# Chosen buffers, eight planned weight chunks and tiles at multiples of 1024 bytes, in an attention and two-layer MLP kernel

## The chip, the cores and the metric

The kernel runs on one core of a Trainium2 chip. The metric is the device time in microseconds (us): the median of three runs before the change is 821.01 us (820.14 to 821.43). The instructions of a core stand in separate queues, one for each engine: TensorE (PE in the rows, with its weight loads as PEld), VectorE (DVE), ScalarE (ACT), GpSimd (POOL) and SyncE (SP), which here issues every DMA. Each engine takes its queue in order.

## The reference

Two batches of eight heads (16 heads in all, of 768 tokens by 64) go through attention in which a query sees only the keys whose six hash bits are the same as its own:

```
mask = q_bucket[:, :, :, None] == k_bucket[:, :, None, :]
scores = scale * np.matmul(q, k.transpose(0, 1, 3, 2))
scores = np.where(mask, scores, -1000000000.0)
attn = exp(scores - max); attn = attn / (sum(attn) + 1e-09)
x = attn @ v                      # 1536 tokens x 512
x = leaky(x @ w_in) @ w_out       # 512 -> 2048 -> 512
h = x @ w_in2;  out = (h * cos(h)) @ w_out2
```

## The kernel before

To keep float32 accuracy, each operand of a matmul is split into a rounded high part (ACT writes it) and a low part, operand minus high part, which DVE or POOL writes.

**Attention.** For each of the 16 heads PE computes hash bits (`bits_mm`, line 268), masked scores for a row maximum (`max_mm`, 284, reduced by DVE in line 290), scores again (`qk`, 361 and 362) and, for each of six key blocks, the product with V (`pv`, 396). Between the last two stand the exponential and the split of its result. A table `LO` of letters chooses the way of each block. At a G, ACT writes exp to `pf` (371) and rounds it to `ph` (379), and POOL subtracts (383). At a V, ACT writes exp to `ph` (368) and once more into PSUM (376), and DVE subtracts (383). `st` is a ring of three PSUM buffers that all of these scores use; a V block holds its buffer until the subtraction is done.

**The MLP.** 96 steps (2 layers, 4 groups of 4 blocks of hidden units, 3 token blocks of 512) each have 12 matmuls of 512 columns for `h` (655), an activation on ACT and DVE, and 12 matmuls for `y` (700), which stand some steps later in PE's order. The weights come as 32 chunks of 1 MB, one for each block of hidden units in a layer, each of them used by three steps. A chunk arrives as 64-bit words and is turned into a high and a low float part in seven pieces (`stages`, 560): ACT (580), four on DVE (581, 582, 583, 573), ACT for the high part (584), POOL for the low part (577). Eight chunks are held at a time: six in the former tiles `at0` to `at3` of attention, two (numbers 6 and 7, and later 14, 15 and so on) in `wx0` to `wx3`.

**What sets the order.** `Plan` is a list scheduler: each piece of work has an engine, a cost, predecessors and a priority (`KEY`, `FIX`, `CHUNK_KEY`), and `order` writes each engine's queue from them. All of attention, the first twelve `h` steps, the first nine `y` steps and the first six weight chunks (`CHUNKS`) go through it. After that `rest` (745) writes the steps in a fixed rhythm, and `tick` (598) starts one piece of weight work in each step. The planner takes a ring's buffers in turn, and a tile pool gives them out in turn.

Of the kernel before, what the change touches and what calls it, by code (L numbers as in the profile page):

```python
# [18 lines left out]
NH = B * H  # L19
# [11 lines left out]
LO = [{0: 'GGGGGG', 1: 'VGVGVV', 2: 'GVGGVG', 12: 'GGGVGV', 13: 'GVGGGG', 14: 'VGVVGV', 15: 'GGVGVV'}.get(n, "VGGGVG") for n in range(NH)]  # L31
CHUNKS = 6
# [3 lines left out]
    load=-118, hi=-28, d2=-23, d3=18, lo=-83, dl=-28, bm=-14.2, bw=-32, db2=-57, db1=-38, mm=-8.1, mr=-25,  # L36
    rt=-10, fl=82, neg=-50, dr=-48, de=-28, qk=0.8, ex=-6, cv=-29, sub=-21, pe=86, pv=4.7, pw=3.2, ev=-15,
    lc=10, rc=27, dw=-3, rr=-17, xm=56, xh=57, xl=20, vload=5, vh=25, vl=1, sv=-10.3, sh=101, sl=26, wload=58,
    w0=45, w1=73, w2=10, w3=62, w4=-37, w5=99, w6=-57, mi=-5, ga=-8, gm=-40, gh=80, gl=-47, mo=56, ye=2,
)  # L40
FIX = {
# [7 lines left out]
}  # L49
CHUNK_KEY = (95.9, 69.7, 115.6, 142.2, 66.7, 109.6, 173.8, 129.6)  # L50
# [3 lines left out]
    mm=0.351, mr=0.953, rt=0.12, fl=0.45, dr=0.75, de=1.3, neg=0.65, qk=0.702, ex=0.81, cv=0.84, subV=0.95, subG=1.87,  # L54
    pe=0.351, pv=0.702, pw=0.351, ev=0.83, lc=0.55, rc=0.18, dw=0.45, rr=0.55, xm=1.85, xh=0.83, xl=1.87,
    vload=0.6, vh=0.83, vl=1.87, sv=1.37, sh=0.75, sl=0.4,
    wload=0.4, w0=1.11, w1=0.69, w2=0.69, w3=0.95, w4=0.95, w5=0.93, w6=2.37,
    hi0=0.52, lo0=0.52, k2=0.83, idt=0.5, bm0=1.0, bw0=0.69, kb0=0.52,
    mi=2.73, ga=0.63, gm=0.68, gh=0.63, glV=0.65, glG=1.3, mo=2.73, ye=0.65,
# [34 lines left out]
class Plan:  # L94
# [4 lines left out]
    def __init__(self, rings, free):  # L99
        self.rings, self.free = rings, dict(free)  # L100
        self.items, self.index = [], {}

    def add(self, name, e, kind, key, fn, after=(), take=None, give=(), cost=None, moe=False):
        deps = [self.index[d] for d in after if d is not None and d in self.index]
        it = dict(name=name, e=e, kind=kind, key=(key, len(self.items)), fn=fn, deps=deps, take=take, give=list(give),
                  cost=COST[kind] if cost is None else cost, out=[], left=len(deps), moe=moe, before=[])
        for d in deps:
            d["out"].append(it)
        self.items.append(it)
        self.index[name] = it  # L110

    def order(self):
        free = {e: self.free.get(e, 0.0) for e in "PVAGQ"}
        ready = {e: [] for e in "PVAGQ"}
        taken = {r: [] for r in self.rings}
# [7 lines left out]
        def start(it):  # L123
            t = max(free[it["e"]], it["at"])
            r = it["take"]
            if r is not None:
                n = len(taken[r]) - self.rings[r]
                if n >= 0:
                    t = max(t, taken[r][n].get("end", 1e9))
            return t  # L130

        while len(done) < len(self.items):
# [26 lines left out]
            if it["take"] is not None:  # L159
                it["slot"] = {}  # L160
                taken[it["take"]].append(it["slot"])
                n = len(taken[it["take"]]) - 1 - self.rings[it["take"]]
                it["before"] = [taken[it["take"]][n]["by"]] if n >= 0 else []
            for g in it["give"]:
                self.index[g]["slot"].update(end=end + 0.06, by=it)
# [9 lines left out]

def attention(tc, ctx, plan, xp, dr_p, XH, XL, AT, VH, VL, YX, qkt, v, proj, cst, fd, more_raws, heads=NH):

    nc = tc.nc
    T, V, A, G, Q = nc.tensor, nc.vector, nc.scalar, nc.gpsimd, nc.sync
    if True:  # L180
        pool = lambda n, b, **kw: ctx.enter_context(tc.tile_pool(name=n, bufs=b, **kw))
        con = pool("con", 1)
        raw_p = pool("raw", 2)
        vraw_p = pool("vraw", 1)
        phi_p = pool("phi", 3)
        plo_p = pool("plo", 3)
        pf_p = pool("pf", 2)
        sm_p = pool("sm", 3)
        sv_p = pool("svp", 1)
        st_ps = pool("st", 3, space=bass.MemoryType.PSUM)  # L190
        pv_ps = pool("pvp", 1, space=bass.MemoryType.PSUM)
        OS = [YX[:, i * S:(i + 1) * S] for i in range(2)]
        RR, XX = (YX[:, i * S:(i + 1) * S] for i in (2, 3))
        LC, RC = (xp.tile([128, 4, C], F32, name=n) for n in ("lc", "rc"))
# [6 lines left out]
        raw = {0: raw_p.tile([128, S], F32, name="raw")}  # L201
# [5 lines left out]
        E = [con.tile([128, S], F32R, name=f"e{i}") for i in range(2)]  # L207
        SV = [con.tile([128, 4, 128], F32R, name=f"sv{i}") for i in range(2)]
# [12 lines left out]
        neg = con.tile([1, S], F32, name="neg")  # L221
        G.memset(neg, -1.0)
        ident = con.tile([128, 128], F32R, name="ident")
# [21 lines left out]
        def load_qk(n):  # L245
            raw[n] = raw_p.tile([128, S], F32, name="raw")
# [33 lines left out]
        def max_mm(n, t):  # L280
            at = AT[n % NR]
            ps = st_ps.tile([128, 2, 512], F32, name="st")
# [4 lines left out]
        def max_red(n, t):  # L287
            if n not in mx:
                mx[n] = sm_p.tile([128, C], F32R, name="mx")
            V.reduce_max(mx[n][:, t:t + 1], mps.pop((n, t))[:, :, 0:HS], axis=AX.XY)  # L290

        def row_mm(n):
            rps[n] = st_ps.tile([128, 2, 512], F32, name="st")
            T.matmul(rps[n][0:C, 0, 0:128], mx.pop(n), ident, start=True, stop=True)

        def row_fin(n):
            ps = rps.pop(n)[0:C, 0, 0:128]
            mts[n] = sm_p.tile([C, 2, 128], F32, name="mt")
# [15 lines left out]
        def load_v(g):  # L314
            vraw[g] = vraw_p.tile([128, C, 4, 64], F32, name="vraw")
# [12 lines left out]
        def sum_v(g):  # L328
            ps = st_ps.tile([128, 2, 512], F32, name="st")
# [11 lines left out]
        def sum_vh(g):  # L341
            ps, dst = sv_parts(g)
            svp[g, 1] = sv_p.tile([128, 2, 2, 64], F32R, name="svt")
# [11 lines left out]
        def qk(n, k):  # L355
            at = AT[n % NR]
            ps = st_ps.tile([128, 2, 512], F32, name="st")
# [7 lines left out]
        def exp(n, k):  # L365
            if LO[n][k] == "V":
                phi[n, k] = phi_p.tile([128, S], F32R, name="ph")
                A.activation(halves(phi[n, k]), sps[n, k], AF.Exp, scale=SCALE)
            else:
                pf[n, k] = halves(pf_p.tile([128, S], F32, name="pf"))  # L370
                A.activation(pf[n, k], sps.pop((n, k)), AF.Exp, scale=SCALE)  # L371

        def exp_cv(n, k):
# [27 lines left out]
        drs = {}  # L401
# [11 lines left out]
        def dr_dma(n):  # L413
            drs[n] = dr_p.tile([1, S], F32, name="dr")
            Q.dma_start(drs[n].rearrange("o (p c) -> (o p) c", c=C), RC[:, n % 4])

        def rr_dma(n):
            r = n % 2 * 64
            Q.dma_start(RR[r:r + 64], drs.pop(n).to_broadcast([64, S]))
# [34 lines left out]
        for h in range(2):  # L454
            plan.add(("hi0", h), "A", "hi0", -40, lambda h=h: hi0(h))
            plan.add(("lo0", h), "V", "lo0", -40, lambda h=h: lo0(h), [("hi0", h)])
# [12 lines left out]
        for n in range(heads):  # L469
# [4 lines left out]
            if n:  # L474
                do("load", n, "Q", load_qk, n, take="raw" if n > 1 else None, after=[("load", n - 1), ("dr", n - 3)])
# [3 lines left out]
                do("lo", n, "G", lo, n, after=[("hi", n)], give=[("load", n)] if n > 1 else ())  # L479
# [41 lines left out]
            do("lc", n, "Q", lc_dma, n, take="lc", after=[("ev", n)])  # L521
            do("rc", n, "V", recip, n, take="rc", after=[("lc", n)], give=[("lc", n)])
            do("dw", n, "Q", dr_dma, n, after=[("rc", n)], give=[("rc", n)])
# [13 lines left out]
        tiles = [[(c * 2 + i) // 3 for i in range(2)] for c in range(CHUNKS)]  # L537
        for c in range(CHUNKS):
            key = CHUNK_KEY[c]
            do("wload", c, "Q", wload, c, key=key - 8, after=[("pw", 11, C - 1), ("wload", c - 1), ("w4", c - 2)])  # L540
            readers = [(x, 12 + t, k) for t in tiles[c] for x in ("qk", "mm") for k in range(C)]
            for j, e in enumerate("AVVVVAG"):
                do(f"w{j}", c, e, fd.piece, c, j, key=key, take="wsc" if j == 0 else None, give=[("w0", c)] if j == 6 else (),
                   after=[("wload", c)] if j == 0 else [(f"w{j - 1}", c)] + (readers if j == 5 else []))


class Weights:


    def __init__(self, tc, sc_pool, src, raws, parts):  # L550
        self.tc, self.src, self.sc_p = tc, src, sc_pool
# [8 lines left out]
    def stages(self, c):  # L560
# [6 lines left out]
        sc = self.sc_p.tile([128, 2 * KT * 128], F32, name="wsc")  # L567
# [54 lines left out]
class Moe:  # L622


    def __init__(self, tc, XH, XL, W, fd, out, YX):
# [3 lines left out]
        self.h, self.gs, self.ys, self.open = {}, {}, {}, None  # L629

    def begin(self, ctx):
        pool = lambda n, b, **kw: ctx.enter_context(self.tc.tile_pool(name=n, bufs=b, reuse_waits="tile", **kw))
        self.t_p = pool("t", 2)
        self.g_p = pool("g", LAG + 1)
        y_p = pool("ysb", 1)
        self.h_ps = pool("h", 4, space=bass.MemoryType.PSUM)
        self.y_ps = pool("y", 1, space=bass.MemoryType.PSUM)
# [9 lines left out]
    def mm_in(self, s):  # L647
        b = self.steps[s][2]
        ps = self.h[s] = self.h_ps.tile([128, TB], F32, name="h")
# [8 lines left out]
    def act(self, s):  # L658
        nc, ps = self.tc.nc, self.h[s]
        g = self.gs[s] = self.t_p.tile([128, TB], F32, name="gf")  # L660
        if self.steps[s][0] == 0:
            nc.scalar.activation(g, ps, AF.Copy, scale=0.01)  # L662
        else:

            ki = self.t_p.tile([128, TB], I32, name="ki")
# [12 lines left out]
    def high(self, s):  # L678
        gh = self.g_p.tile([128, TB], F32R, name="gh")
        gl = self.g_p.tile([128, TB], F32R, name="gl")  # L680
# [9 lines left out]
    def mm_out(self, s):  # L690
# [4 lines left out]
        if j == 0:  # L695
            self.ys[l, b] = [self.y_ps.tile([128, TB], F32, name=f"y{e}") for e in range(KT)]
        for e in range(KT):
            y = self.ys[l, b][e]
# [160 lines left out]
```

## Time and profile before

| | us |
|---|---|
| median of 3 runs | 821.01 |
| the profiled execution's own time | 821.24 |
| its span, from first to last instruction | 819.4 |
| busy: PE / DVE / ACT / POOL | 786.8 / 479.5 / 438.4 / 432.4 |
| first `h` matmul of the MLP starts at | 264.84 |
| last matmul starts at | 815.25 |

A step's length is read from the distance of the starts of its first matmuls, since the durations of single matmuls overlap.

### The profile page before, as it was taken

To read this page: it belongs to the slowest core of one execution; us is meant where nothing else is said; L and a number is where in the kernel's file an instruction comes from. 1 tells how busy PE (TensorE), PEld (TensorE's weight loads), DVE (VectorE), ACT (ScalarE), POOL (GpSimd) and SP (SyncE) were. 2 spreads that over 40 slices of the span, in tenths; PEclk is the share of its full clock that TensorE was granted. 3 is DMA by queue.
4 is the path that set the end of the run, shared out by engine and by line. 5 is a ranking of instruction groups with operands and counts; after the bars stand their busy time and mean duration, and the time that the engine had idled before them with its cause. 6 is when DMAs were issued, how large, how long until landed. Compare 5 with 4: busy or idle time off the path is not lost. (4 is left out here: it accounts for less than half of the span.)

```text
span 819.4 us, 9862 instructions
## 1 busy us (share of the span) xinstructions
PE 786.8 (96%) x3648; PEld 667.8 (81%) x3648; DVE 479.5 (59%) x579; ACT 438.4 (53%) x630; POOL 432.4 (53%) x282
## 2 busy tenths in 40 slices
PE   6999999999899999779999999999999999999998
PEld 4899999989799788558888888887788888888886
DVE  7666666656777952337666356456747737743333
ACT  3777878867789424224333224355656555544442
POOL 8768887977778512223455334846623533532221
PEclk9999999999999999889999999999999999999999
DMA  6534534524531610112222112102202210000012
GB/s 177 149 84 111 147 91 102 138 64 109 167 110 57 215 68 1 52 52 90 70 98 103 52 52 102 52 4 100 102 1 66 89 52 1 0 1 2 0 52 103
DMA packets 24264, 63.19 MB, mean 77 GB/s; under 512 B 7684, under 2 KB 11428, under 8 KB 20120
## 3 DMA queue, kind: packets, MB, share of 16 engines
q1 hardware_dynamic: 24216, 62.56, 25.1%
q8 instruction: 29, 0.48, 0.2%
q14 instruction: 19, 0.16, 0.1%
HBM read 46.21 MB, written 3.19 MB: 60 GB/s over the span
## 5 line engine op out<-in xcount | busy, mean ns | idle before, releaser
L687 POOL TENSOR_TENSOR gl<-gf,gh 128x512 fp32r<-128x512 f32 x88 | 123.1, 1399 | 298.8 <-ACT gh L681 238.0
L700 PE MATMUL y<-gh,at 128*128 128x512 f32 x576 | 181.0, 395 | 1.6 <-ACT ys L709 1.6
L655 PE MATMUL h<-XH,at 128*128 128x512 f32 x576 | 143.9, 391 | 0.0
L383 POOL TENSOR_TENSOR pl<-pf,ph 128x768 fp32r<-128x768 f32 x62 | 116.3, 1884 | 40.1 <-ACT ph L379 33.3
L700 PEld LDWEIGHTS y<-gh,at 128*128 128x128 f32 x576 | 107.6, 187 | 28.1 <-ACT ys L709 2.0
L655 PEld LDWEIGHTS h<-XH,at 128*128 128x128 f32 x576 | 108.0, 188 | 24.9 <-POOL at L577 0.5
L290 DVE TENSOR_REDUCE mx<-st 128x1 fp32r<-128x768 f32 x96 | 90.9, 956 | 43.4 <-PE st L284 41.4
L700 PE MATMUL y<-gl,at 128*128 128x512 f32 x288 | 113.6, 395 | 0.7 <-POOL gl L687 0.7
L662 ACT ACTIVATE gf<-h 128x512 f32<-128x512 f32 x48 | 28.7, 598 | 143.1 <-PE h L655 127.0
L672 DVE TENSOR_TENSOR gf<-h,gf 128x512 f32<-128x512 f32 x48 | 33.1, 690 | 108.7 <-ACT gf L662 108.6
L666 ACT ACTIVATE ki<-h 128x512 int32<-128x512 f32 x48 | 28.7, 598 | 107.1 <-PE h L655 107.1
L655 PE MATMUL h<-XL,at 128*128 128x512 f32 x288 | 77.0, 389 | 0.0
L667 DVE SCALAR_TENSOR_TENSOR gf<-ki,h 128x512 f32<-128x512 int32 x48 | 33.0, 687 | 72.9 <-ACT ki L666 66.9
L361 PE MATMUL st<-at 77*128 77x384 f32 x192 | 67.4, 351 | 3.8 <-DVE mx L290 2.3
L700 PEld LDWEIGHTS y<-gl,at 128*128 128x128 f32 x288 | 53.9, 187 | 14.3 <-POOL gl L687 1.1
L362 PE MATMUL st<-at 128*128 128x384 f32 x192 | 65.2, 340 | 0.0
L577 POOL TENSOR_TENSOR at<-wsc,at 128x1024 fp32r<-128x1024 f32 x24 | 60.3, 2512 | 7.1 <-ACT at L584 7.1
L655 PE MATMUL h<-XH,wx 128*128 128x512 f32 x192 | 52.6, 417 | 11.2 <-ACT wx L584 10.5
L655 PEld LDWEIGHTS h<-XL,at 128*128 128x128 f32 x288 | 54.1, 188 | 11.4
L681 ACT ACTIVATE gh<-gf 128x512 fp32r<-128x512 f32 x96 | 59.8, 623 | 4.0 <-DVE gf L672 2.3
L371 ACT ACTIVATE pf<-st 128x768 f32<-128x768 f32 x62 | 50.1, 808 | 19.3 <-PE st L362 17.6
L676 DVE SCALAR_TENSOR_TENSOR gf<-gf,h 128x512 f32<-128x512 f32 x48 | 32.9, 685 | 46.2 <-ACT gf L675 46.2
(95 smaller groups left out, 1467.1 us busy)
## 6 DMA issues: line engine op xcount, KB each, us to landing
wrvh<-in_w_dram SPq DMA_DIRECT2D x16, 1024.0 KB
wrvl<-in_w_dram SPq DMA_DIRECT2D x16, 1024.0 KB
at<-at SPq DMA_DIRECT2D x63, 192.0 KB
raw<-in_qk_dram SPq DMA_DIRECT2D x15, 384.0 KB
vraw<-in_v_dram SPq DMA_DIRECT2D x4, 768.0 KB
yx<-dr SPq DMA_DIRECT2D x16, 192.0 KB
out_dram<-ys SPq DMA_DIRECT2D x6, 256.0 KB
out_dram<-yx SPq DMA_DIRECT2D x6, 256.0 KB
```

Source lines behind the costliest of these rows:

```text
L290: V.reduce_max(mx[n][:, t:t + 1], mps.pop((n, t))[:, :, 0:HS], axis=AX.XY)
L361: T.matmul(o, at[0:R76 + 1, 2, kc], at[0:R76 + 1, 0, COL[h]], start=True, stop=False)
L362: T.matmul(o, at[:, 3, kc], at[:, 1, COL[h]], start=False, stop=True)
L371: A.activation(pf[n, k], sps.pop((n, k)), AF.Exp, scale=SCALE)
L383: (V if LO[n][k] == "V" else G).tensor_tensor(halves(plo[n, k]), pf.pop((n, k)), halves(f32(phi[n, k])), op=ALU.subtract)
L577: G.tensor_tensor(lf, sc, f32(hf), op=ALU.subtract)
L655: self.tc.nc.tensor.matmul(ps, w[:, 0, k], x[:, k, cols], start=(j == 0), stop=(j == 3 * KT - 1))
L667: nc.vector.scalar_tensor_tensor(g, ki, -TWOPI, ps, op0=ALU.mult, op1=ALU.add)
L672: nc.vector.tensor_tensor(g, ps, g, op=ALU.max)
L681: self.tc.nc.scalar.activation(gh, self.gs[s], AF.Copy)
L687: (nc.vector if s < GLV else nc.gpsimd).tensor_tensor(gl, g, f32(gh), op=ALU.subtract)
L700: self.tc.nc.tensor.matmul(y, w[:, 1, e], x, start=(j == 0 and i == 0), stop=(j == GRP - 1 and i == 2))
```

## The change

The priorities (`KEY`, `FIX`, `CHUNK_KEY`) and some of the planner's costs are other numbers. `LO` has 53 V blocks of 96, where it had 34; most heads now have four V blocks and two G blocks, where they had two and four. `CHUNKS` is 8. Chunks 6 and 7 are loaded after the last `pv` of attention.

The planner gives each taker the buffer that is free first, and the kernel uses that very buffer (`plan.tile`), so rings are no longer taken in turn. The MLP's tiles are plain lists, taken by step number as the pools gave them.

The addresses move, since a tile `sums` of 1920 bytes (it holds `LC` and `RC`) is the first, and the small tiles stand at the end. In bytes past a multiple of 1024, a partition's tiles begin at:

| tile | before | after |
|---|---|---|
| `XH`, `XL`, `at0`-`at3`, `vh`, `vl` | 128 | 0 |
| `gh`, `gl`, `gf`, `ki`, `wsc`, `ys`, `wx0`-`wx3` | 320 | 0 |
| `raw`, `ph`, `pl`, `pf` | 608 | 0 |

Within them, weight blocks lie 512 bytes apart, and a step's columns of `XH` begin at multiples of 2048.

```
-LO = [{0: 'GGGGGG', 1: 'VGVGVV', 2: 'GVGGVG', 12: 'GGGVGV', ...}.get(n, "VGGGVG") for n in range(NH)]
-CHUNKS = 6
+LO = [{0: 'GGGVGG', 1: 'VGGGVG', 2: 'GGVGVG', 11: 'GGGVGV', ...}.get(n, "VGVGVV") for n in range(NH)]
+CHUNKS = 8
-            r = it["take"]
-            if r is not None:
-                n = len(taken[r]) - self.rings[r]
-                if n >= 0:
-                    t = max(t, taken[r][n].get("end", 1e9))
+            if it["take"] is not None:
+                t = max(t, min(end for end, _ in places[it["take"]]))
...
+                j = it["place"] = min(range(len(ring)), key=lambda j: ring[j][0])
...
-            ps = st_ps.tile([128, 2, 512], F32, name="st")
+            ps = plan.tile("st")
...
-            do("wload", c, "Q", wload, c, key=key - 8, after=[("pw", 11, C - 1), ("wload", c - 1), ("w4", c - 2)])
+            do("wload", c, "Q", wload, c, key=key - 8, after=[("pw", 11 if c < 6 else NH - 1, C - 1), ("wload", c - 1), ("w4", c - (2 if c < 6 else 4))])
...
-        self.t_p = pool("t", 2)
-        self.g_p = pool("g", LAG + 1)
+        self.GF, self.KI = one(t_p, "gf", 2), one(t_p, "ki", 2, I32)
+        self.GH, self.GL = one(g_p, "gh", LAG + 1, F32R), one(g_p, "gl", LAG + 1, F32R)
...
+        sums = xp.tile([128, 480], F32, name="sums")
         XH = xp.tile([128, KT, NT], F32R, name="XH")
```

**POOL where the MLP begins, before.** The `wx` rows are the low parts of chunks 6 and 7; `gl` are the low parts of the steps, eight of which are on DVE.

```order
L432 TENSOR_TENSOR XL<-yx,XH 128x768
L577 TENSOR_TENSOR at_70<-wsc,at_69 128x1024
L577 TENSOR_TENSOR at_70<-wsc,at_70 128x1024
L687 TENSOR_TENSOR gl<-gf,gh 128x512 x5
L577 TENSOR_TENSOR wx_2911<-wsc,wx_2910 128x1024
L687 TENSOR_TENSOR gl<-gf,gh 128x512
L577 TENSOR_TENSOR wx_2913<-wsc,wx_2912 128x1024
```

**The same place after.**

```order
L439 TENSOR_TENSOR XL<-yx,XH 128x768
L585 TENSOR_TENSOR at_71<-wsc_78,at_71 128x1024
L585 TENSOR_TENSOR at_71<-wsc_77,at_70 128x1024
L585 TENSOR_TENSOR wx_2358<-wsc_78,wx_2357 128x1024
L585 TENSOR_TENSOR wx_2356<-wsc_77,wx_2355 128x1024
L695 TENSOR_TENSOR gl_2334<-gf_2326,gh_2330 128x512
```

Chunks 6 and 7 stand ahead of POOL's first `gl`, the one of step 8, where they stood behind five and six of them.

**DVE at the end of attention, before.** `pl<-st,ph` are the last V subtractions; rows on `wsc` are weight pieces, from `wrvh` of chunk 2 and from `wrvl` of chunk 3; the first `gf` belongs to the MLP.

```order
L573 SCALAR_TENSOR_TENSOR wsc<-wrvh_2332,wsc 128x1024
L383 TENSOR_TENSOR pl<-st,ph 128x768
L411 RECIPROCAL rc<-lc 128x6
L383 TENSOR_TENSOR pl<-st,ph 128x768
L581 TENSOR_SCALAR wsc<-wsc 128x1024
L582 TENSOR_SCALAR wsc<-wsc 128x1024
L583 SCALAR_TENSOR_TENSOR wsc<-wrvl_2333,wsc 128x1024
L672 TENSOR_TENSOR gf<-h,gf 128x512
L573 SCALAR_TENSOR_TENSOR wsc<-wrvl_2333,wsc 128x1024
```

**The same place after.**

```order
L392 TENSOR_TENSOR plo_91<-st_110,phi_89 128x768
L589 TENSOR_SCALAR wsc_78<-wsc_78 128x1024
L590 TENSOR_SCALAR wsc_78<-wsc_78 128x1024
L392 TENSOR_TENSOR plo_92<-st_108,phi_90 128x768
L419 RECIPROCAL sums<-sums 128x6
L591 SCALAR_TENSOR_TENSOR wsc_78<-wrvl_1887,wsc_78 128x1024
L392 TENSOR_TENSOR plo_93<-st_109,phi_88 128x768
L392 TENSOR_TENSOR plo_91<-st_110,phi_89 128x768
L581 SCALAR_TENSOR_TENSOR wsc_78<-wrvl_1887,wsc_78 128x1024
L419 RECIPROCAL sums<-sums 128x6
L681 TENSOR_TENSOR gf_2326<-h_2338,gf_2326 128x512
```

The four pieces of chunk 3 now stand among the last subtractions, ahead of the first `gf`; three of them stand ahead of the last two subtractions.

**SP at the start, before and after.** `vraw` is the load of V for the first four heads.

```order
L447 DMA at_70<-neg 1x16x48
L316 DMA vraw<-in_v_dram 128x6x256
L258 DMA at_67<-at_67 64x768 x2
L247 DMA raw<-in_qk_dram 128x768
```

```order
L454 DMA at_71<-neg 1x6x128
L267 DMA at_68<-at_68 64x768 x2
L325 DMA vraw_87<-in_v_dram 128x6x256
L256 DMA raw_85<-in_qk_dram 128x768
```

The load of V now stands behind two copies of the first head's split parts.

## Rows read from the trace of the kernel before

**Rows 1.** The page, part 1: busy us, share of the span, count.

```profile
PE 786.8 (96%) x3648; PEld 667.8 (81%) x3648; DVE 479.5 (59%) x579; ACT 438.4 (53%) x630; POOL 432.4 (53%) x282
```

**Rows 2.** Waits of PE: us in total, times, longest us.

```profile
PE h L655 <- ACT wx L584: 10.5, 2, 5.8
...
PE st L361 <- DVE mx L290: 2.3, 1, 2.3
PE st L284 <- ACT pf L371: 2.0, 2, 1.8
PE y L700 <- ACT ys L709: 1.6, 1, 1.6
```

**Rows 3.** Stretches: from:to, length, busy us (count) by engine, clock, DMA.

```profile
200.00:264.00 64.00, 59.50 (x324) 56.94 (x322) 47.32 (x54) 52.12 (x67) 49.89 (x25) 0.97 0.33 100
...
224.60:228.00 3.40, 3.40 (x12) 3.40 (x12) 3.33 (x5) 1.51 (x2) 0.19 (x1) 0.50 0.91 345
337.20:344.00 6.80, 4.58 (x10) 3.18 (x11) 0.71 (x1) 1.06 (x1) 2.36 (x1) 0.50 0.47 154
```

**Rows 4.** Timeline round chunks 6 and 7: start, us, engine, line, [idle before <-releaser].

```profile
333.94 0.40 PE L700 MATMUL y<-gl,at 128*128 128x512 f32 x1
...
337.95 1.06 ACT L584 ACTIVATE wx<-wsc 128x1024 fp32r<-128x1024 f32 x1 [5.19 <-DVE wsc L573]
...
339.06 2.07 PE L655 MATMUL h<-XH,wx 128*128 128x512 f32 x4 [4.71 <-ACT wx L584]
...
344.64 0.62 PE L700 MATMUL y<-gh,at 128*128 128x512 f32 x2
...
347.20 0.39 PE L700 MATMUL y<-gl,at 128*128 128x512 f32 x1
...
353.38 2.07 PE L655 MATMUL h<-XH,wx 128*128 128x512 f32 x4 [5.79 <-ACT wx L584]
...
358.63 0.62 PE L700 MATMUL y<-gh,at 128*128 128x512 f32 x2
```

**Rows 5.** Timeline of PE in the MLP: starts of steps, and the last matmul.

```profile
264.84 2.01 PE L655 MATMUL h<-XH,at 128*128 128x512 f32 x8
...
289.98 1.98 PE L655 MATMUL h<-XH,at 128*128 128x512 f32 x8
...
292.70 1.98 PE L655 MATMUL h<-XH,at 128*128 128x512 f32 x8
...
311.90 0.63 PE L700 MATMUL y<-gh,at 128*128 128x512 f32 x2
...
314.70 0.63 PE L700 MATMUL y<-gh,at 128*128 128x512 f32 x2
...
812.76 0.62 PE L700 MATMUL y<-gh,wx 128*128 128x512 f32 x2
...
815.25 0.39 PE L700 MATMUL y<-gl,wx 128*128 128x512 f32 x1
```

**Rows 6.** Groups of line 383: xcount, busy us, mean ns, idle before.

```profile
L383 POOL TENSOR_TENSOR pl<-pf,ph 128x768 fp32r<-128x768 f32 x62 | 116.3, 1884 | 40.1 <-ACT ph L379 33.3 <-DMA raw<-in_qk_dram 1.9 <-PE st L284 1.7
...
L383 DVE TENSOR_TENSOR pl<-st,ph 128x768 fp32r<-128x768 f32 x34 | 32.5, 956 | 15.7 <-ACT st L376 14.6 <-POOL pl L383 0.4 <-POOL XL L432 0.3
```

**Rows 7.** Timeline where the MLP first needs the last head.

```profile
283.31 1.86 POOL L432 TENSOR_TENSOR XL<-yx,XH 128x768 fp32r<-128x768 f32 x1 [0.96 <-ACT XH L429]
...
286.35 1.07 PE L655 MATMUL h<-XL,at 128*128 128x512 f32 x4
```

**Rows 8.** Timeline of the start.

```profile
6.70 2.34 SPq L258 DMA_DIRECT2D at<-at  x2
...
12.30 1.58 ACT L322 ACTIVATE vh<-vraw 128x768 fp32r<-128x768 f32 x2 [1.17 <-DMA vraw<-in_v_dram]
```

**Rows 9.** Waits of DVE: us in total, times, longest us.

```profile
DVE mx L290 <- PE st L284: 41.4, 56, 2.9
...
DVE pl L383 <- ACT st L376: 14.6, 21, 2.9
```

More of the change, by code (lines that the diff above doesn't have):

```diff
@@ L100, in __init__, with tile @@
         self.rings, self.free = rings, dict(free)
-        self.items, self.index = [], {}
+        self.items, self.index, self.tiles, self.place = [], {}, {}, 0
+    def tile(self, ring):
+        return self.tiles[ring][self.place]
     def add(self, name, e, kind, key, fn, after=(), take=None, give=(), cost=None, moe=False):
@@ L105, in add @@
         it = dict(name=name, e=e, kind=kind, key=(key, len(self.items)), fn=fn, deps=deps, take=take, give=list(give),
-                  cost=COST[kind] if cost is None else cost, out=[], left=len(deps), moe=moe, before=[])
+                  cost=COST[kind] if cost is None else cost, out=[], left=len(deps), moe=moe, before=[], place=0)
         for d in deps:
@@ L114, in order @@
         ready = {e: [] for e in "PVAGQ"}
-        taken = {r: [] for r in self.rings}
+        places = {r: [(0.0, None)] * k for r, k in self.rings.items()}
         wire = port = 0.0
@@ L159, in order @@
             if it["take"] is not None:
[L160 to L163, printed above, removed]
+                ring = places[it["take"]]
+                j = it["place"] = min(range(len(ring)), key=lambda j: ring[j][0])
+                it["before"] = [ring[j][1]] if ring[j][1] else []
+                ring[j] = (1e9, None)
             for g in it["give"]:
-                self.index[g]["slot"].update(end=end + 0.06, by=it)
+                g = self.index[g]
+                places[g["take"]][g["place"]] = (end + 0.06, it)
             for o in it["out"]:
@@ L173, in order, with attention @@
         return done
-def attention(tc, ctx, plan, xp, dr_p, XH, XL, AT, VH, VL, YX, qkt, v, proj, cst, fd, more_raws, heads=NH):
+def attention(tc, ctx, plan, sums, dr_p, XH, XL, AT, VH, VL, YX, qkt, v, proj, cst, fd, more_raws, heads=NH):
     nc = tc.nc
@@ L182, in attention, with ring @@
         con = pool("con", 1)
[L183 to L191, printed above, removed]
+        psum = pool("psum", 1, space=bass.MemoryType.PSUM)
+        def ring(name, shape, dtype=F32, p=con):
+            plan.tiles[name] = [p.tile(shape, dtype, name=f"{name}{i}") for i in range(plan.rings[name])]
+        ring("raw", [128, S])
+        ring("vraw", [128, C, 4, 64])
+        ring("phi", [128, S], F32R)
+        ring("plo", [128, S], F32R)
+        ring("pf", [128, S])
+        E = [con.tile([128, S], F32R, name=f"e{i}") for i in range(2)]
+        SV = [con.tile([128, 4, 128], F32R, name=f"sv{i}") for i in range(2)]
+        ring("svt", [128, 2, 2, 64], F32R)
+        ring("mt", [C, 2, 128])
+        ident = con.tile([128, 128], F32R, name="ident")
+        ring("mx", [128, C], F32R)
+        ring("st", [128, 2, 512], p=psum)
+        ring("pv", [128, 2, 512], p=psum)
+        DR = [dr_p.tile([1, S], F32, name=f"dr{i}") for i in range(4)]
         OS = [YX[:, i * S:(i + 1) * S] for i in range(2)]
         RR, XX = (YX[:, i * S:(i + 1) * S] for i in (2, 3))
-        LC, RC = (xp.tile([128, 4, C], F32, name=n) for n in ("lc", "rc"))
+        LC, RC = (sums[:, i * 4 * C:(i + 1) * 4 * C].rearrange("p (a b) -> p a b", b=C) for i in range(2))
         cs = con.tile([128, 130], F32, name="cs")
@@ L200, in attention @@
         Q.dma_start(pj[64:128], proj)
-        raw = {0: raw_p.tile([128, S], F32, name="raw")}
+        raw = {0: plan.tiles["raw"][0]}
         COL = [slice(h * HS, (h + 1) * HS) for h in range(2)]
@@ L281, in max_mm @@
             at = AT[n % NR]
-            ps = st_ps.tile([128, 2, 512], F32, name="st")
+            ps = plan.tile("st")
             for h in range(2):
@@ L328, in sum_v @@
         def sum_v(g):
-            ps = st_ps.tile([128, 2, 512], F32, name="st")
+            ps = plan.tile("st")
             vs = (VH[g % 2], VL[g % 2])
@@ L356, in qk @@
             at = AT[n % NR]
-            ps = st_ps.tile([128, 2, 512], F32, name="st")
+            ps = plan.tile("st")
             kc = slice(k * 128, (k + 1) * 128)
@@ L454, in attention @@
         for h in range(2):
-            plan.add(("hi0", h), "A", "hi0", -40, lambda h=h: hi0(h))
-            plan.add(("lo0", h), "V", "lo0", -40, lambda h=h: lo0(h), [("hi0", h)])
+            plan.add(("hi0", h), "A", "hi0", -40, lambda h=h: hi0(h), take=None if h else "raw")
+            plan.add(("lo0", h), "V", "lo0", -40, lambda h=h: lo0(h), [("hi0", h)], give=[("hi0", 0)] if h else ())
         plan.add(("hi", 0), "A", "k2", -39, lambda: A.activation(AT[0][U, 2], f32(AT[0][L, 0]), AF.Copy), [("hi0", 0), ("hi0", 1)])
@@ L474, in attention @@
             if n:
-                do("load", n, "Q", load_qk, n, take="raw" if n > 1 else None, after=[("load", n - 1), ("dr", n - 3)])
+                do("load", n, "Q", load_qk, n, take="raw", after=[("hi0", 0), ("load", n - 1), ("dr", n - 3)])
                 do("hi", n, "A", hi, n, after=[("load", n)] + old)
@@ L478, in attention @@
                 do("d3", n, "Q", at_dma, n, U, 3, L, 0, after=[("hi", n)] + old)
-                do("lo", n, "G", lo, n, after=[("hi", n)], give=[("load", n)] if n > 1 else ())
+                do("lo", n, "G", lo, n, after=[("hi", n)], give=[("load", n)])
                 do("dl", n, "Q", at_dma, n, L, 3, L, 1, after=[("lo", n)])
@@ L535, in wload @@
             fd.load(c + 1)
-        tiles = [[(c * 2 + i) // 3 for i in range(2)] for c in range(CHUNKS)]
         for c in range(CHUNKS):
             key = CHUNK_KEY[c]
-            do("wload", c, "Q", wload, c, key=key - 8, after=[("pw", 11, C - 1), ("wload", c - 1), ("w4", c - 2)])
-            readers = [(x, 12 + t, k) for t in tiles[c] for x in ("qk", "mm") for k in range(C)]
+            do("wload", c, "Q", wload, c, key=key - 8, after=[("pw", 11 if c < 6 else NH - 1, C - 1), ("wload", c - 1), ("w4", c - (2 if c < 6 else 4))])
+            heads_ = [12 + (c * 2 + i) // 3 for i in range(2)]
+            readers = [(x, h, k) for h in heads_ for x in ("qk", "mm") for k in range(C)]
             for j, e in enumerate("AVVVVAG"):
-                do(f"w{j}", c, e, fd.piece, c, j, key=key, take="wsc" if j == 0 else None, give=[("w0", c)] if j == 6 else (),
-                   after=[("wload", c)] if j == 0 else [(f"w{j - 1}", c)] + (readers if j == 5 else []))
+                do(f"w{j}", c, e, fd.piece, c, j, key=key,
+                   after=[("wload", c), ("w0", c - 1), ("w6", c - 2)] if j == 0 else [(f"w{j - 1}", c)] + (readers if j == 5 else []))
 class Weights:
     def __init__(self, tc, sc_pool, src, raws, parts):
-        self.tc, self.src, self.sc_p = tc, src, sc_pool
+        self.tc, self.src = tc, src
+        self.sc = [sc_pool.tile([128, 2 * KT * 128], F32, name=f"wsc{i}") for i in range(2)]
         self.raws, self.parts = raws, parts
@@ L678, in high @@
     def high(self, s):
-        gh = self.g_p.tile([128, TB], F32R, name="gh")
-        gl = self.g_p.tile([128, TB], F32R, name="gl")
+        gh, gl = (t[s % (LAG + 1)] for t in (self.GH, self.GL))
         self.tc.nc.scalar.activation(gh, self.gs[s], AF.Copy)
@@ L694, in mm_out @@
         j = f % GRP
-        if j == 0:
-            self.ys[l, b] = [self.y_ps.tile([128, TB], F32, name=f"y{e}") for e in range(KT)]
         for e in range(KT):
-            y = self.ys[l, b][e]
+            y = self.YP[e]
             for i, (w, x) in enumerate(((wh, gh), (wl, gh), (wh, gl))):
@@ L730, in plan @@
             x = [("xl", n) for n in range(1, H if b == 0 else NH, 2)]
-            do("mi", "P", self.mm_in, s, take="h", after=[("w6", f), ("w5", f), ("pw", NH - 1, C - 1), ("mi", s - 1)] + x)
-            do("ga", "A", self.act, s, take="t", after=[("mi", s)])
-            do("gm", "V", self.act_mid, s, after=[("ga", s)], give=[("mi", s)])
-            do("gh", "A", self.high, s, take="g", after=[("gm", s)])
+            do("mi", "P", self.mm_in, s, after=[("w6", f), ("w5", f), ("pw", NH - 1, C - 1), ("mi", s - 1), ("gm", s - 4)] + x)
+            do("ga", "A", self.act, s, after=[("mi", s), ("gl", s - 2), ("ga", s - 1)])
+            do("gm", "V", self.act_mid, s, after=[("ga", s)])
+            do("gh", "A", self.high, s, after=[("gm", s), ("mo", s - LAG - 1)])
             e = "V" if s < GLV else "G"
-            do("gl", e, self.low, s, after=[("gh", s)], give=[("ga", s)], cost=COST["gl" + e])
+            do("gl", e, self.low, s, after=[("gh", s)], cost=COST["gl" + e])
             if e == "V":
@@ L740, in plan @@
                 end = f % GRP == GRP - 1
-                do("mo", "P", self.mm_out, s, take="y" if f % GRP == 0 else None, give=[("gh", s)], after=[("gl", s), ("mo", s - 1)])
+                do("mo", "P", self.mm_out, s, after=[("gl", s), ("mo", s - 1)] + [("ye", s - 1, j) for j in range(KT)])
                 for j in range(KT if end else 0):
-                    do("ye", "AV"[j % 2], self.evac, s, j, j=(j,), after=[("mo", s)], give=[("mo", s - GRP + 1)] if j == KT - 1 else ())
+                    do("ye", "AV"[j % 2], self.evac, s, j, j=(j,), after=[("mo", s)])
     def rest(self):
@@ L808, in emit @@
                 seen.add(id(it))
+                plan.place = it["place"]
                 it["fn"]()
```

85 lines of the change are left out of this document (40 added, 45 removed), and 15 rows, old and new, of the table FIX.

## The prediction

> **What bounds the kernel now.** I read the page's busy times first: PE is busy for 786.8 of 819.4 us [rows 1], so the most that waits can give back is about 33 us, and anything beyond that must come from matmuls that run closer together. Then I read the waits of PE [rows 2], the clock in the stretches round them [rows 3], the timeline of the longest [rows 4], and last the distances between the starts of steps, where no wait is shown at all [rows 5]. The reader is to see three things.
>
> First, the longest waits are two, 10.5 us together, for ACT's high part of a weight chunk in `wx` [rows 2]. Each comes after a y step: PE starts that step's last matmul at 333.94 and starts its next y step at 344.64, with one h step between; the same happens from 347.20 to 358.63 [rows 4]. ACT itself waited for DVE, and its row ends 0.05 us before the matmul starts. Behind such a wait PE runs at half speed: the granted clock is 0.50, the 1.2 GHz level, from 337.2 to 344.0 [rows 3].
>
> Second, equal work does not take equal time in the MLP. An h step that follows an h step takes 292.70 - 289.98 = 2.72 us. A y step with weights in `at` takes 314.70 - 311.90 = 2.80 us. The last y step, with weights in `wx`, takes 815.25 - 812.76 plus one matmul of 0.227, again 2.72 us [rows 5]. All have twelve matmuls of the same shape. What differs is where the two operands begin: 128 and 128 bytes past a multiple of 1024 in the first case, 128 and 320 in the second, 320 and 320 in the third. Equal offsets run at 2.72, unequal ones at 2.80.
>
> Third, attention ends at 264.84 [rows 5] and is a packed stretch with a few waits: 2.3 us for a maximum on DVE and 2.0 us for an exponential on ACT [rows 2]. A half-clock stretch of 3.4 us like the one from 224.6 to 228.0 [rows 3] stands behind each of the two, and costs 1.7 us since PE was busy all through it.
>
> **The change part by part.** The sums are made against the profiled execution, 821.24 us, which is 0.23 above the median of 821.01 and 1.8 above its own span.
>
> *Chunks 6 and 7 are planned.* A wait with its aftermath is the distance in rows 4 less what belongs there, one y matmul and an h step, 0.23 + 2.72 = 2.95 us. That gives 10.70 - 2.95 = 7.75 and 11.43 - 2.95 = 8.48, together 16.2 us, half clock included. By the order, POOL now writes the low parts of both chunks ahead of its first `gl`, that of step 8, while the chunks are first read in steps 14 and 15. Between lie PE's remaining planned steps, at least ten of 2.72 us, or 27 us; two chunks' work by the rows of before is hidden under those. I take all 16.2. The bound on the other side is 0, if the loads, which now wait for the last `pv`, come too late; a gain above 16.2 is excluded, since nothing else waits there. The DVE and ACT pieces of the two chunks stand among the activations of steps 3 to 7; what is late next would be a y step of these, and the three h steps or more that PE holds between an h step and its y cover that.
>
> *All large tiles begin at multiples of 1024.* From the first h matmul to the last matmul PE needs 815.25 - 264.84 = 550.4 us. The 192 steps at 2.72, less the last matmul, would be 522.0. The excess is 28.4; less the 16.2 and the 1.6 us wait for `ys` [rows 2] 10.6 us are left, as an upper bound. The lower bound for a gain by equal offsets are the y steps on `at` weights alone, three quarters of 96, 72 x 0.08 = 5.8 us. I take 9.0: the h steps on `wx` weights are unequal too, and an h step behind a y step has to settle, but some of the 10.6 is small waits. No row shows offset 0 paired with 0, so the outer bounds are 0 and 10.6.
>
> The Trainium skill says otherwise ("SBUF — State Buffer", "Who interferes with whom"): the matmul's moving operand and the weight load have independent read ports, and "PE and ACT never wait on anyone". By that rule the tiles' addresses are of no consequence, and this term would be 0 in place of 9.0. The trace of before does not agree, with 2.80 beside 2.72 for the same work [rows 5]; what it can't show is whether the offsets are the cause. The rule is the first rival below.
>
> *Nineteen blocks go from G to V.* POOL loses 19 x 1.884 = 35.8 us and DVE gains 19 x 0.956 = 18.2 us [rows 6]; ACT has two passes either way. PE's work is the same. Together with the choice of free buffers this only pays where PE waits: at most the 2.3 + 2.0 us and the two half-clock stretches of 1.7, 7.7 us in all. A new order has its own waits in place of these, and no row tells them, so I take a quarter, 2 us. The bounds are a gain of 7.7 and a loss of 19 x (0.956 + 14.6 / 21) = 31 us, if every added subtraction with its wait [rows 9] were passed on to PE.
>
> *The start.* The load of V is issued behind two copies of the first head, whose issue ends at 6.70 + 2.34 = 9.04 [rows 8]; ACT, which splits V at 12.30, was waiting for it. The sums over V thus come up to 3 us later, and in the new order PE has the third head's hash bits behind them. Some of it lies beside other waits of the start; 0 to 3 us, I take 1.
>
> *The joint.* The last head's low part ends at 283.31 + 1.86 = 285.17, and PE reads it from 286.35 [rows 7], so there is 1.2 us to spare. PE has four h and three y steps ahead of that point in both orders, but they will be some 0.5 us shorter, and DVE has chunk 3's pieces ahead of its last subtractions. SP still issues two weight loads of 1 MB between that head's small DMAs; one such load takes 3 us at the 345 GB/s of rows 3, so a shift by one of them costs 3 less the 1.2, and with a half-clock stretch 3.5. Between 0 and 3.5 I take 1, nearer to the order of before.
>
> The 1.6 us wait for `ys` stands where the layers meet, in code whose order is the same; I leave it. Sum: 821.24 - 16.2 - 9.0 - 2 + 1 + 1 = 796.0; for the median 0.2 less. I forecast 796.
>
> **The rivals.** *The offsets do nothing (0.15).* The steps' 2.80 may come from the rhythm of weights and moving columns in h and y rather than from addresses. For it: y and h differ in more than the tile. Against it: the same y code runs at 2.72 with `wx` weights [rows 5]. Time 796 + 9 = 805.
>
> *Attention sheds all its waits (0.20).* POOL, until now the most delayed splitter at 1884 ns a block [rows 6], gets 36 us lighter, and a buffer that is free is taken whatever its turn. If all 7.7 us go and the start and the joint cost nothing, it is 796 - 5.7 - 2 = 788.
>
> *The chunk wait moves and stays (0.05).* This is the case in which the change doesn't do what it says: the loads of chunks 6 and 7 wait for the last `pv` and stand in SP's queue between the small DMAs of the last head; if PE still waits for both, the time is 796 + 16 = 812.
>
> *DVE becomes the bound of attention, and it is slower (0.05).* DVE is busy for 47.32 of 64 us at the end of attention [rows 3], and waits there lie in front of it as well: 0.7 us for each of 21 subtractions, 0.74 for each of 56 maxima [rows 9]. With 19 more subtractions, four in most heads, and chunk 3 brought ahead, its queue may be the last thing that each head waits for, since `st` buffers are held until it is done. The price is up to 31 us as worked out above, 827; it decides once more than 25 of these 31 reach PE, some four fifths. Against it: 64 - 47.32 leaves 16.7 us free where four blocks and one chunk are added.
>
> **How the numbers follow.** The forecast has 0.55. Its own range is 791 to 801: attention may give its 7.7 or lose some 5, and the offsets may be worth 5.8 to 10.6. The stated range, 785 to 809, takes in the first two rivals with some microseconds on either side, and leaves out the last two and the tails. A difference under 0.2%, 1.6 us, can't be told from no change. The forecast and the first three rivals hold 0.95 and are faster, but for 0.01 at the edge of the third; the DVE rival gives 0.04 slower, and 0.01 within 0.2% where its price just meets the gains. That makes 0.94 faster, 0.02 the same and 0.04 slower.
>
> **What would show it.** The waits of PE should hold no `wx` row above 1 us, and the clock should be 1.00 throughout the MLP. A y step on `at` weights should take 2.72 us from start to start; 2.80 makes the offsets wrong. The first h matmul should start between 259 and 268; later than 275 means that DVE bounds attention, and its waits will then be for ACT no more, while PE's will be for `pl` and `mx`. A wait in front of the fifth h step would show the joint. The forecast is wrong above all if 2.80 stays, or if attention ends more than 8 us from 264.

## The result, and the profile after

The changed kernel takes 795.28 us (median of 4 runs, 794.38 to 797.66), the kernel before 821.22 beside it: a ratio of 0.969, with a 95% interval of 0.967 to 0.971. 796 was forecast. The profiled execution took 795.2 us, 26.0 less than that of before, and its trace splits them. The first h matmul starts at 263.67 in place of 264.84 [rows 5], so attention gave 1.2 us. From there to the start of the last matmul it was 550.4 us and is now 789.30 - 263.67 = 525.6, so the MLP gave 24.8. Its first matmul and its last:

```profile
263.67 2.01 PE L664 MATMUL h<-XH,at 128*128 128x512 f32 x8
...
789.30 0.39 PE L706 MATMUL y<-gl,wx 128*128 128x512 f32 x1
```

First the page's busy times, which answer to [rows 1]:

```profile
PE 772.6 (97%) x3648; PEld 665.2 (84%) x3648; DVE 474.9 (60%) x598; ACT 435.5 (55%) x630; POOL 409.7 (52%) x263
```

The same 3648 matmuls keep PE busy for 14.2 us less: more than half of the 26.0 are not waits that went, but matmuls that run faster, at their full clock or closer together. Then PE's waits (engine, line, what it waited for: us in total, times, longest), which answer to [rows 2]:

```profile
PE st L277 <- DVE pb L230: 6.5, 2, 6.1
PE y L706 <- ACT ys L715: 1.7, 1, 1.7
PE st L370 <- ACT pf L380: 1.5, 2, 0.9
PE st L342 <- POOL vl L335: 1.2, 1, 1.2
PE st L370 <- DVE plo L392: 1.2, 1, 1.2
...
PE st L370 <- DVE at L283: 0.8, 1, 0.8
```

There is no row for `wx` any more. The first row, a wait at the very start, was 6.7 us before. The rows for `vl` (the start) and `plo` (the end of attention) are new. The stretches that answer to [rows 3], with the granted clock behind POOL's column:

```profile
200.00:264.00 64.00, 59.67 (x319) 54.32 (x319) 51.45 (x58) 51.89 (x67) 39.93 (x22) 1.00 0.38 124
...
337.20:344.00 6.80, 6.80 (x32) 5.63 (x31) 5.36 (x6) 2.67 (x5) 2.77 (x3) 1.00 0.41 154
```

At the end of attention POOL fell from 49.89 to 39.93 us and DVE rose from 47.32 to 51.45, as the nineteen blocks ask. From 337.2 to 344.0 the clock is 1.00, the 2.4 GHz level, where it was 0.50. Last, the starts of PE's steps, which answer to [rows 5] (start, duration of the group, instruction):

```profile
288.18 1.98 PE L664 MATMUL h<-XH,at 128*128 128x512 f32 x8
...
290.90 1.98 PE L664 MATMUL h<-XH,at 128*128 128x512 f32 x8
...
304.50 0.62 PE L706 MATMUL y<-gh,at 128*128 128x512 f32 x2
...
307.22 0.61 PE L706 MATMUL y<-gh,at 128*128 128x512 f32 x2
```

An h step is 290.90 - 288.18 = 2.72 us as before, and a y step on `at` weights 307.22 - 304.50 = 2.72 where it was 2.80. That holds for all 72 y steps on `at` but the two that wait where the layers meet.

### The profile page after: what moved, and what is told of

Its sections match the earlier page's. It is cut to its first block, busy times and chain, and to the rows that moved or that the text cites. A ratio compares the mean times of both kernels' runs of the same rounds, so it can differ in the third digit from the quotient of the medians.

```text
span 793.4 us, 9934 instructions
## 1 busy us (share of the span) xinstructions
PE 772.6 (97%) x3648; PEld 665.2 (84%) x3648; DVE 474.9 (60%) x598; ACT 435.5 (55%) x630; POOL 409.7 (52%) x263
## 5 line engine op out<-in xcount | busy, mean ns | idle before, releaser
L695 POOL TENSOR_TENSOR gl<-gf,gh 128x512 fp32r<-128x512 f32 x88 | 134.7, 1531 | 264.4 <-ACT gh L689 200.6
L706 PE MATMUL y<-gh,at 128*128 128x512 f32 x576 | 177.7, 390 | 1.9 <-ACT ys L715 1.7
L664 PE MATMUL h<-XH,at 128*128 128x512 f32 x576 | 142.3, 389 | 0.0
L706 PEld LDWEIGHTS y<-gh,at 128*128 128x128 f32 x576 | 107.9, 188 | 25.2 <-ACT ys L715 2.2
L392 POOL TENSOR_TENSOR plo<-pf,phi 128x768 fp32r<-128x768 f32 x43 | 80.8, 1883 | 55.7 <-ACT phi L388 49.8
L706 PE MATMUL y<-gh,wx 128*128 128x512 f32 x192 | 59.1, 389 | 0.0
L392 DVE TENSOR_TENSOR plo<-st,phi 128x768 fp32r<-128x768 f32 x53 | 50.3, 952 | 9.1 <-ACT st L385 7.2
```

The lines of the kernel that those rows point to most:

```text
L664: self.tc.nc.tensor.matmul(ps, w[:, 0, k], x[:, k, cols], start=(j == 0), stop=(j == 3 * KT - 1))
L695: (nc.vector if s < GLV else nc.gpsimd).tensor_tensor(gl, g, f32(gh), op=ALU.subtract)
L706: self.tc.nc.tensor.matmul(y, w[:, 1, e], x, start=(j == 0 and i == 0), stop=(j == GRP - 1 and i == 2))
```

## The experiments

In what follows "excess" is what the MLP's 191 distances from step to step hold beyond 2.722 us each, summed from the trace: 28.0 us before, 3.2 after.

**Offsets alone.** The order is that of before, on every engine:

```
+sums = [xp.tile([128, 4, C], F32, name=n) for n in ("lc", "rc")]   # ahead of XH
-LC, RC = (xp.tile([128, 4, C], F32, name=n) for n in ("lc", "rc"))  # behind YX
+LC, RC = xp   # attention is given sums in the place of xp
```

> The kernel before, with its order untouched; only lc and rc are allocated ahead of XH, so that every operand of the MLP begins at 320 bytes past a multiple of 1024, none at a multiple. Theory (equal offsets): y steps on `at` weights fall from 2.80 to 2.72 us, the two `wx` stalls of 7.75 and 8.48 us stay, 821.2 - 9.0 = 812.2 us (810.6 to 815.4 by the bounds of the term). Rival 1 (offsets do nothing, the planned order does it): 2.80 and 821. Rival 2 (the start at a multiple of 1024 counts, not equality): no faster than 821, and h steps on `at` weights at 2.80 as well, some 826.

It took 813.88 us against 820.4, ratio 0.993 (0.991 to 0.995). A y step on `at` weights is 2.72 us:

```profile
305.66 0.61 PE L700 MATMUL y<-gh,at 128*128 128x512 f32 x2
...
308.38 0.61 PE L700 MATMUL y<-gh,at 128*128 128x512 f32 x2
```

Rival 1 is out, since nothing was reordered, and rival 2 too, since no operand begins at a multiple of 1024. The excess fell by 6.6 us, not 9. The two stalls swallow part of the rest: PE starts the y step in front of the first of them at 330.14, 1.2 us earlier than before (331.38), and the y step behind the second at 358.78, no earlier than before (358.63). The four steps of the stalls hold 17.7 us beyond 2.722 each, where they held 16.4. One h step at 275.34 that takes 3.12 us holds another 0.4. With these 1.7 the offsets are worth some 8.3, and 9 was too much.

**All at 320, in the changed kernel.**

```
-sums = xp.tile([128, 480], F32, name="sums")
+sums = xp.tile([128, 48], F32, name="sums")
```

> The changed kernel with the tile of the sums cut from 1920 to 192 bytes, so that all large tiles begin at 320 past a multiple of 1024. Theory (equality counts): 2.72 us a step everywhere, 795.3 us. Rival 2 (multiples of 1024 count): steps of 2.80, 795.3 + 192 x 0.08 = 811 at most, 801 if only the y steps on `at` weights suffer.

793.48 us, 2.72 in every kind of step, excess 3.2. Multiples of 1024 are not what counts.

**The MLP's own tiles shifted.** One unused tile is put in front of gf, gh, gl, ys and wx; here with 192 bytes, the difference of before:

```
 t_p, g_p, y_p = pool("t", 1), pool("g", 1), pool("ysb", 1)
+t_p.tile([128, 48], F32, name="fill")
```

> The changed kernel with 192 bytes left free in front of the MLP's own tiles, so that gh, gl and wx begin at 192 and XH, XL and the weights in `at` at 0; attention's tiles stay. Theory: y steps on `at` weights 2.80 us, 72 x 0.08 = 5.8 us at the least and 9.0 by the term of the prediction, 801 to 804 us. Rival 1: 2.72 and 795.3.

801.87 us, ratio 0.979 (0.976 to 0.982), and the 2.80 is back:

```profile
306.86 0.63 PE L707 MATMUL y<-gh,at 128*128 128x512 f32 x2
...
309.66 0.63 PE L707 MATMUL y<-gh,at 128*128 128x512 f32 x2
```

The excess is 11.6 us, so with the chunks planned the offsets are worth 8.4.

**Other differences of the two operands' offsets**, one run each (in the table below, 0 and 192 have four):

> As the shift by 192 bytes, with 64: gh, gl and wx begin at 64, XH, XL and the weights in `at` at 0. Theory (any difference of the two operands' offsets costs): y steps on `at` weights 2.80 us. Rival (what matters is how far the difference is from a multiple of 512, half of a weight tile's row or more): between 2.72 and 2.80, near 2.74.

> As the shift by 192 bytes, with 128. Theory (any difference costs): 2.80 us a y step on `at` weights. Rival (it grows with the distance to a multiple of 512): some 2.77.

> As the shift by 192 bytes, with 256. Theory (any difference costs): 2.80 us a y step on `at` weights. Rival (it grows with the distance to a multiple of 512): more than the 2.80 of 192, some 2.83.

> As the shift by 192 bytes, with 512, half of the 1024 that the change aims at. Theory (only equal offsets modulo 1024 are free): 2.80 us a y step on `at` weights, 801 to 804 us. Rival (a row of a weight tile is 512 bytes, so the difference counts modulo 512 or less): 2.72 and 795.

| shift, bytes | 0 | 64 | 128 | 192 | 256 | 512 |
|---|---|---|---|---|---|---|
| y step on `at`, median us | 2.72 | 2.76 | 2.79 | 2.80 | 2.72 | 2.72 |
| h step on `wx`, median us | 2.72 | 2.80 | 2.79 | 2.77 | 2.72 | 2.72 |
| excess, us | 3.2 | 11.7 | 11.5 | 11.6 | 3.2 | 3.2 |
| time, us | 795.3 | 800.4 | 800.0 | 801.9 | 791.8 | 798.0 |

My theory that any difference costs fell at 256 and 512, and the rival that the cost grows up to 256 fell at 256. What the runs show is that a difference by 256 or 512 bytes is free, as 0 is, and that 64, 128 and 192 cost alike in the sum. Step by step they do not. A shift by 64 puts the moving operand of a y step on `at` 64 bytes ahead of its weights, and that of an h step on `wx` 64 bytes behind them. Counted as moving operand minus weights, modulo 256, the table's two rows agree: 64 gives 2.76 (y at 64) and 2.77 (h at 192), 128 gives 2.79 twice, 192 gives 2.80 twice. The sums come out alike because steps with equal offsets that stand between slow ones are slower too: an h step on `at` behind a y step on `at` has a median of 2.77 us at 64 and 2.74 at 128 and 192. Why 256 stays open. The times of the last two columns differ by 6 us at equal excess; that is attention's doing, and comes below.

**Six chunks.**

```
-CHUNKS = 8
+CHUNKS = 6
```

> The changed kernel with six planned chunks in place of eight, all else as it is. Theory: the two waits for `wx` come back in front of the y steps on chunks 6 and 7 with the half clock behind them, 795.3 + 16.2 = 811.5 us. Rival (the stalls came from the old order of the chunks before, and buffers and order alone would have removed them): no wait over 1 us for `wx`, 795.

811.68 us, ratio 0.990 (0.987 to 0.993). The wait is back as in [rows 2]:

```profile
PE h L664 <- ACT wx L592: 10.4, 2, 5.8
```

That is 16.4 us above the changed kernel by the medians, and 17.4 by the excess (20.6 against 3.2).

**The old numbers.** The changed kernel with the old LO, keys, chunk keys and costs, and eight chunks.

> The changed kernel (its buffers, offsets and eight chunks) with the old numbers of the plan: the old LO with 62 blocks on POOL, the old keys, chunk keys and costs. Theory (attention was bound by PE before and after, so that blocks, keys and buffers are worth little): the first h step starts within 5 us of 264, 792 to 800 us. Rival (the new planner's choice of buffers only pays with numbers found for it): the first h step starts later than 269 and the time is 801 or more.

808.86 us, ratio 0.984 (0.981 to 0.988), and the first h step starts at 280.52. The MLP's excess is 3.9, so attention alone lost its 17 us. At its end (200 to 264 us) PE's clock is 0.89 and new waits stand in front of PE:

```profile
PE pv L404 <- POOL plo L391: 2.7, 2, 2.2
PE st L302 <- DVE mx L298: 2.3, 3, 1.6
```

Near the start PE works through 13.7 us at half clock, which the profile after does not have; at that clock 12.82 busy us cost, as an estimate, 6.4 more than at full clock:

```profile
21.50:35.20 13.70, 12.82 (x40) 11.59 (x40) 6.30 (x7) 7.77 (x11) 6.58 (x5) 0.50 0.70 182
```

My theory fell and the rival holds: the free choice of buffers does not pay with any numbers, and attention is bound by PE only as long as an order keeps it so. No run has the new numbers under the old planner, or the new `LO` alone, so what the choice of buffers and the nineteen blocks are worth by themselves stays open.

**Where attention's spread comes from.** In nine profiles with the attention of the changed kernel the first h step starts between 260.24 and 266.49. At the end of attention DVE's integer piece of chunk 0 (L591) meets POOL's XL (L439). With the shift by 512:

```profile
238.94 3.37 DVE L591 SCALAR_TENSOR_TENSOR wsc<-wrvh,wsc 128x1024 int32<-128x1024 int32 x1
...
239.39 1.84 POOL L439 TENSOR_TENSOR XL<-yx,XH 128x768 fp32r<-128x768 f32 x1
...
243.23 0.53 PE L370 MATMUL st<-at 77*128 77x384 f32 x1 [1.36 <-DVE plo L392]
```

and with the shift by 256, the same instructions on every engine up to there:

```profile
235.73 1.58 DVE L591 SCALAR_TENSOR_TENSOR wsc<-wrvh,wsc 128x1024 int32<-128x1024 int32 x1
...
236.18 2.82 POOL L439 TENSOR_TENSOR XL<-yx,XH 128x768 fp32r<-128x768 f32 x1
```

One of the two takes its usual time, and the other its own plus most of the first's. DVE lost in four of the nine profiles, with the first h step at 263.7 to 266.5, and won in five, with 260.2 to 263.3. The Trainium skill ("SBUF — State Buffer", "SBUF: two separate sides") has the rule: a DVE instruction with two SBUF inputs and a POOL instruction that reads SBUF need the same pair of ports, and whichever "starts first gets the pair for the whole instruction; the other fully blocks". The trace agrees on the blocking (3.37 us for 1.58, 2.82 for 1.84); by its records DVE starts 0.45 us ahead both times, so that the recorded starts do not tell who wins.

The collision is only part of the spread. From the start of DVE's piece to the first h step it is 24.5 to 24.7 us in the five profiles in which DVE won and 26.0 to 28.9 in the four in which it lost, so losing costs some 1.3 to 4.4 us, half clock included. But the piece itself starts anywhere from 235.69 to 238.94, and these 3.2 us stand ahead of the collision. They are there early: PE's 281st matmul starts between 65.9 and 69.0. Half clock from 25.0 to 31.8 is in one of these starts, the shift by 512, and the wait for `vl` is 0.6 to 1.5 us; what sets the rest is not shown.

The run that takes the collision away moves one POOL instruction:

```
+behind(("xl", 11), ("sub", 14, 1))   # in the finished order, XL goes behind the next `plo`
```

> The changed kernel with one POOL instruction moved: the low part of heads 10 and 11 into XL goes behind the first low part of head 14 on POOL, so that it no longer starts 0.45 us after DVE's integer piece of chunk 0. In the profiled runs so far that piece took 1.6 us in four and 3.4 us in four, with the same order of instructions, and only with 3.4 did PE wait 1.2 to 1.5 us for `plo` behind it. Theory (the two engines hold each other up, and who is first is a matter of chance): the piece takes 1.6 us every time, no wait for `plo`, no half clock behind it, 2 to 3 us less than the changed kernel in half of its runs: 792 to 794 us. Rival (the 3.4 us are not POOL's doing, or the next collision takes its place): 795.

793.18 us, ratio 0.966 (0.963 to 0.969). The piece took 1.59 us, PE's `st` matmuls no longer wait for `plo` (waits of 0.2 us are left in front of `pv`), and from the piece to the first h step it is 24.6 us, as where DVE had won. To judge the 2 us, the changed kernel ran once more:

> The changed kernel itself once more, unaltered, to compare with the move on POOL, whose four runs lay at 792.1 to 794.6 with a ratio of 0.966 to the kernel before. Theory (in the changed kernel DVE's piece and POOL's low part collide, and chance decides who is first): runs spread over 792 to 798, median 794.5 to 796, ratio near 0.969; in the profile the piece takes either 1.6 us with no wait for `plo`, or 3.4 us with a wait of 1.2 to 1.5 us behind it. Rival (the move gains nothing, and what it seemed to gain is the spread between runs): median 793.2, ratio 0.966.

797.27 us, ratio 0.972 (0.970 to 0.974), above the 0.966 of the move. But the interval of the move meets that of the changed kernel's first measurement, 0.969, and that of the run with all tiles at 320, 0.9675 (0.966 to 0.969), which has the changed kernel's order and no move. So the trace shows that the move takes the collision away, and the times don't show a gain: it lies between nothing and 4 us, by the run that one compares with.

In this run's profile DVE had won (1.58 us), where the same program had lost in the profile after. Its profiled execution is 3.5 us behind that of the move from other places. The first h step comes 1.8 us later, and DVE's piece starts late already, at 238.71. The MLP's excess is 4.8 against 3.2: a stretch of half clock stands behind the `ys` wait, which is 1.68 us here. The profile after waits 1.73 at that place and keeps its clock. Here, and in the profile after:

```profile
561.50:564.90 3.40, 3.40 (x9) 2.63 (x8) 3.37 (x4) 1.56 (x3) 3.40 (x2) 0.50 0.00 0
```

```profile
560.00:564.00 4.00, 3.25 (x14) 2.48 (x14) 3.76 (x5) 3.40 (x7) 4.00 (x3) 1.00 0.16 66
```

**The load of V as well.**

```
+behind(("vload", 0), ("load", 1))   # ahead of the two copies
```

> As the move on POOL, and the load of V is issued ahead of the two copies of the first head, behind the load of the second head. Theory (T4: the load stands behind a copy that waits for DVE until 8.3 us): the sums over V are no longer waited for (0.7 to 1.5 us at 18 us) and PE keeps its clock there, 1 to 2 us less than with the move on POOL alone: 790 to 793 us. Rival (something else is late then: the second head's own load beside 768 KB more in the queues, or the copies behind it): no gain, or 1 us lost.

792.95 us, ratio 0.966 (0.963 to 0.969). The wait for `vl` fell from 0.7 to 0.2 us, and the first h step came 0.4 us earlier than with the move alone (261.00 against 261.44): no gain that the times can tell. The rival has something for it: PE's wait for `at` behind L283 rose from 0.9 to 1.4 us, and a new one of 0.6 for `sv` stands there.

## Why the prediction was right, and which terms were off

- **Chunks 6 and 7, forecast 16.2.** Right. With unequal offsets in both, the excess goes from 28.0 to 11.6, which is 16.4; with equal offsets, from 21.4 to 3.2, which is 18.2. These pairs differ in the whole plan; the run that changes the number of chunks alone gives 17.4, more than the 16.2 that I had called the most. The cause is as forecast, and the size depends on the offsets: with faster steps PE comes to the same late weights earlier and waits longer.
- **Offsets, forecast 9.0 within 5.8 to 10.6.** Right in cause, 0.6 too high: 8.4 with the chunks planned, 6.6 without, since the stalls then take part of it back. In either order of counting the two terms make 24.8, the whole gain of the MLP, as they must between the same two ends. I had not said that they interact. Equality was too narrow a reading: 256 or 512 between the two will do. And it is not a rule for every matmul: in attention `ph` begins at 608 and `vh` at 128 before and both at 0 after, and successive `pv` matmuls of 384 columns start 0.17 to 0.18 us apart, by the medians, in both.
- **The first rival, 805,** is out: with the order unchanged, the place of two small tiles moved a y step from 2.80 to 2.72. With it falls the reading that I gave the Trainium skill ("SBUF — State Buffer", "Who interferes with whom"). Its sentence that PE never waits on anyone is about one engine waiting for another, and no run here shows PE held up in that way; but the moving operand and the weight load, whose ports it calls independent, are not independent in time here, 2.72 against 2.80 us by their addresses alone. By what mechanism is not shown.
- **Attention, forecast a gain of 2 less 1 for the start: 1.** Measured 1.2 in this profile, but a step was mis-sized. I took a quarter of 7.7 because no row told the new order's waits. Nine profiles put the same order between a gain of 4.6 and a loss of 1.65, and the old numbers under the new buffers lose 17. The term was the difference of large things, and near to 1 because an order for these buffers was found, not because little was at stake. That the whole sum came within 1 us is luck in part: the same kernel took 797.27 us when it was measured again. Nor do the bounds given for 791 to 801 add up to it: attention's 7.7 gained or 5 lost and offsets of 10.6 or 5.8 give 789 and 806. The two splitter groups answer to [rows 6]:

```profile
L392 POOL TENSOR_TENSOR plo<-pf,phi 128x768 fp32r<-128x768 f32 x43 | 80.8, 1883 | 55.7 <-ACT phi L388 49.8
...
L392 DVE TENSOR_TENSOR plo<-st,phi 128x768 fp32r<-128x768 f32 x53 | 50.3, 952 | 9.1 <-ACT st L385 7.2
```

- **The start, forecast a loss of 1.** The sums over V now wait 1.2 us for `vl`; issuing the load earlier cut such a wait by half a microsecond.
- **The joint, forecast a loss of 1.** It cost nothing. The last head's XL ends on POOL at 280.43 + 1.85 = 282.28, and the fifth h step, which reads it from 284.56, follows the third y step without a gap:

```profile
280.43 1.85 POOL L439 TENSOR_TENSOR XL<-yx,XH 128x768 fp32r<-128x768 f32 x1 [0.96 <-ACT XH L436]
```

```profile
282.74 1.98 PE L664 MATMUL h<-XH,at 128*128 128x512 f32 x8
284.56 1.07 PE L664 MATMUL h<-XL,at 128*128 128x512 f32 x4
```

- **The other rivals.** Attention did not shed its waits (`pf` 1.5, `plo` 1.2 and `at` 0.8 us are left), though in the best profiles it ended 3.4 us earlier than in this one. The chunk wait did not stay, and DVE, with 51.45 of 64 us busy, did not become the bound. Sum by terms: -16.4 - 8.4 - 1.2 makes the 26.0 us, where 25.2 was forecast. The attention term in it is that of one profile.

## What to carry to other kernels

Compare the start-to-start distance of equal matmul groups, not only the waits: a stall of 0.08 us in each of 72 steps has no row among the waits, and was cured by where two small tiles lie. Two gains in front of one wait do not add up while that wait stands, so price each with and without the other. Numbers found for one planner need not be a start for another (they cost 17 us here), and where two engines meet and chance decides who goes first, one measurement of the order's time is not good to a microsecond.

## What the hardware showed that I had not expected

- Unequal offsets of moving operand and weights cost matmuls of 512 columns 8.3 to 8.5 us of excess at 64, 128 and 192 bytes and nothing at 256 and 512. The single step does depend on the distance, counted with its sign modulo 256: 2.76 to 2.77 us at 64, 2.79 at 128, 2.80 at 192, against 2.72.
- Where DVE and POOL collide, the order does not settle who goes first: the changed kernel lost DVE's piece in one profile (3.35 us) and won it in the other (1.58). With the shift by 512, one 1.36 us wait of PE that follows was paid again in half clock: the matmuls from 243.23 on started 0.32 us apart in place of 0.18.
- A wait of 1.7 us at the same place left the clock at 1.00 in one run, and in another the clock was at 0.50 from 561.5 to 564.9.
